# All head pairs turned on VectorE from long-run loads: a hashed attention followed by a channel mix on one core

## Chip, cores, metric

The kernel runs on one core of a Trainium2 chip. The metric is the device time of one execution in microseconds (us). A measurement is the median of several runs; profiles are of one execution.

## What is computed

Inputs q, k, v are 4 batches x 8 heads x 768 tokens x 64 values in float32. Each token of q and k gets a 6-bit bucket from the signs of six projections; attention runs only between tokens of one bucket. The result, with heads side by side (512 values per token), goes through a channel mix with a one-token shift.

```python
q_bits = (np.einsum('bhsd,dk->bhsk', q, proj) > 0)
mask = q_bucket[:, :, :, None] == k_bucket[:, :, None, :]
scores = np.where(mask, scale * (q @ k.T), -1e9)          # then softmax, then @ v
x = attn_out.transpose(0, 2, 1, 3).reshape(B, S, H * D)
x_prev = concatenate([zeros, x[:, :-1]], axis=1)
xk = mu_k * x + (1 - mu_k) * x_prev                        # xr alike, with mu_r
k = maximum(xk @ w_k, 0); v = k * k @ w_v                  # 512 -> 1024 -> 512
out = sigmoid(xr @ w_r) * v
```

## The kernel before

**Staging.** Two heads form a pair: 16 pairs, four per batch. A pair takes twelve slots, one for each head j and each block jc of 128 keys. The loop at L698 goes through all 192 slots; in each it records, for all engines, the score of that slot (`score`, L382: two matmuls and one exponential on ScalarE, L396), the product with v of the slot two earlier (`pv`, L404), some matmuls of the channel mix of the batch before (`ffn`, L580, from a list that is filled at slot 6 of the first pair of batches 1 to 3), and the steps that make later pairs ready. This text writes (n, s) for slot s of pair n. Every engine executes its own instructions in the order in which the loop recorded them, and so do the DMA queues of SP and ScalarE. After the loop come the rest of the list and the channel mix of the last batch, the tail.

**Masking by signs.** A score matmul contracts 64 values of a head and, in six further rows of the same operands (`augs`, called aq and ak in the profile), the signs of the projections as plus or minus a half. `bits` (L342) makes them: four matmuls of the turned pair with `projp`, one VectorE step to plus or minus a half into `sg`, and eight small SP DMAs (L360) that store six rows each into the operands.

**Turning.** q and k come in with tokens on partitions and must be turned to values on partitions (tile `t`). Pairs 0 to 3 (`NTE = 4`) are loaded naturally (`load_qk`, L235: 128 partitions of six tokens) and turned by TensorE transposes and bank copies (`turn_pe`, L305). Pairs 4 to 15 are loaded in blocks (`load_blocks`, L255) and turned by two VectorE transposes of 32 x 32 blocks (`turn_dve`, L326), with casts on GpSimd (L333). A block load puts, for one head and one half e of the 64 values, 32 rows of four runs of 352 values into 32 partitions; there are eight such DMAs a pair. `load_v` (L274) brings v of a pair in one DMA. Loads of pair n + 3 and of v of pair n + 2 stand at (n, 3).

**Output side.** `turn_out` (L437) turns a finished pair's result with TensorE into a PSUM bank, copies it to `xt`, and copies one column group for the shift. `mix` (L454) makes xk and xr of it in five VectorE steps. `rv_items` (L529) ends in `os` (L540) and one SP DMA of 128 rows x 2 KB. Squares (`norm`, L282) bound the scores; at the end a flag chooses a general path, which these inputs do not take.

**Weights** come through GpSimd's software queue (`load_w`, L591) at (0, 2), (0, 8), (1, 0), (1, 6), (1, 10) and (2, 10).

Of the kernel before, what the change touches and what calls it, by code (L numbers as in the profile page):

```python
# [9 lines left out]
FP32 = mybir.dt.float32  # L10
# [23 lines left out]
def kernel(  # L34
# [24 lines left out]
    NTE = 4  # L59
# [9 lines left out]
    projp = consts.tile([P, 32], FP32, name="projp")  # L69
# [99 lines left out]
    def fast():  # L169
        with ExitStack() as fx:  # L170
# [3 lines left out]
            nat = pool("nat", 3)  # L174
            blkp = pool("blk", 2)
            vfp = pool("vf", 3)
# [4 lines left out]
            ptp = pool("pt", 6)  # L181
# [9 lines left out]
            osp = pool("os", 4)  # L191
# [26 lines left out]
            nats, blks, vfs, pts, obs, xts, t32s, oos = ({} for _ in range(8))  # L218
# [16 lines left out]
            def load_qk(n):  # L235
                b, t = divmod(n, NPB)
                tl = nat.tile([P, 2, 2, HALF], FP32, name=f"qk{n}", tag="qk")
                nats[n] = tl
                if n == 0:
                    for j in range(2):  # L240
                        for i, eng in enumerate((nc.sync, nc.scalar)):
                            eng.dma_start(
                                out=tl[:, i, j, :],
                                in_=SRC[i][b, 2 * t + j].rearrange("(p c) d -> p (c d)", c=NC_),
                            )
                    return
                for i in range(2):
                    nc.sync.dma_start(
                        out=tl[:, i, :, :],
                        in_=SRC[i][b, 2 * t : 2 * t + 2].rearrange(  # L250
                            "j (p c) d -> p j (c d)", c=NC_
                        ),
                    )

            def load_blocks(n):  # L255

                b, t = divmod(n, NPB)
                tl = blkp.tile([P, 2, 4, HALF], FP32, name=f"bl{n}", tag="bl")
                blks[n] = tl
                w = HALF - D // 2  # L260
                for i in range(2):
                    for j in range(2):
                        src = SRC[i][b, 2 * t + j].rearrange("(f r c) d -> r f (c d)", f=4, c=NC_)
                        for e in range(2):
                            g = 2 * j + e
# [5 lines left out]
            def load_pair(n):  # L271
                (load_qk if n < NTE else load_blocks)(n)

            def load_v(n):  # L274
                b, t = divmod(n, NPB)
                vf = vfp.tile([P, 2, S // 2], FP32, name=f"vf{n}", tag="vf")
                nc.sync.dma_start(
                    out=vf, in_=v[b, 2 * t : 2 * t + 2].rearrange("j (p c) d -> p j (c d)", c=NC_)
                )
                vfs[n] = vf  # L280

            def norm(n, i, eng):  # L282

                if n < NTE:
                    src = nats[n][:, i].rearrange("p j f -> p (j f)")
                    shape = [P, S]
                else:
                    src = blks[n][:, i].rearrange("p f (c x) -> p (f c) x", x=D)[:, :, 0 : D // 2]
                    shape = [P, 4 * NC_, D // 2]
# [15 lines left out]
            def turn_pe(n, i, j, which):  # L305

                tp = bank(which, [P, HALF], FP32, f"tp{n}_{i}_{j}")
                for x in range(3):
                    cols = slice(x * P, (x + 1) * P)
                    nc.tensor.transpose(tp[:, cols], nats[n][:, i, j, cols], ident32)  # L310
                dst = t32(n)[:, i, j, :]
                if n == 0 and i == 1:
                    nc.scalar.copy(dst, tp)
                else:
                    nc.vector.tensor_copy(dst, tp)
                for e in range(2):
                    (nc.gpsimd, nc.vector)[e ^ j].tensor_scalar(
                        out=augs[n % NSET]["qk"[i], j][ROWS[j], e * HALF : (e + 1) * HALF],
                        in0=dst[ROWS[e], :],
                        scalar1=(1.0, ALPHA)[i],  # L320
                        scalar2=1.0,
                        op0=ALU.mult,
                        op1=ALU.mult,
                    )

            def turn_dve(n, i):  # L326
                src = blks[n][:, i].rearrange("p f (c x) -> p c f x", x=D)[:, :, :, 0 : D // 2]
                nc.vector.transpose(  # L328
                    t32(n)[:, i].rearrange("p h (c f x) -> p (h c) f x", c=3, f=4), src
                )  # L330

            def cast(n, i, j, eng):
                eng.tensor_scalar(  # L333
                    out=augs[n % NSET]["qk"[i], j][ROWS[j], :],
                    in0=t32(n)[ROWS[j], i].rearrange("p h y -> p (h y)"),
                    scalar1=(1.0, ALPHA)[i],
                    scalar2=1.0,
                    op0=ALU.mult,
                    op1=ALU.mult,
                )  # L340

            def bits(n, js, which, two_queues=False):  # L342


                bb = bank(which, [64 * len(js), HALF], FP32, f"bb{n}_{js[0]}")
                for g, (x, i) in enumerate((x, i) for x in js for i in range(2)):
                    nc.tensor.matmul(  # L347
                        bb[32 * g : 32 * g + 32, :], projp, t32(n)[:, i, x, :],
                        start=True, stop=True,
                    )  # L350
                sg = sgp.tile([64 * len(js), HALF], BF16, name=f"sg{n}_{js[0]}", tag="sg")
# [3 lines left out]
                for g, (x, i) in enumerate((x, i) for x in js for i in range(2)):  # L355
                    eng = nc.scalar if two_queues and i else nc.sync
                    for y in range(2):
                        j, e = (x, y) if n < NTE else (y, x)
                        r = 32 * g + NB * y
                        eng.dma_start(  # L360
# [3 lines left out]
                            in_=sg[r : r + NB, :],  # L364
                        )

            def values(n, j):
                vf = vfs[n][:, j, :]
                va, vs = vas[n % NSET][j], vss[n % NSET][j]
                if n < NTE:  # L370
                    to = va[:, :, 0:D].rearrange("p (e c) d -> p e c d", e=2)
                    of = vf.rearrange("p (c e d) -> p e c d", e=2, d=D)
                else:
                    to, of = va[:, :, 0:D], vf.rearrange("p (c d) -> p c d", d=D)
# [62 lines left out]
            def turn_out(n, which):  # L437
                b, t = divmod(n, NPB)
                xt = xtp.tile([P, P + S], BF16, name=f"xt{n}", tag=f"xt{t}")
                ot = bank(which, [P, S], BF16, f"ot{n}")  # L440

                for i in range(NC_):
                    c = 2 * (i % 3) + i // 3 if n < NTE else i
                    nc.tensor.transpose(ot[:, c * P : (c + 1) * P], obs[n][:, i, :], ident16)  # L444
                nc.vector.tensor_copy(xt[:, P : P + S], ot)  # L445
                xts[b, t] = xt

                nc.vector.memset(xt[:, 0:1], 0.0)
                nc.vector.tensor_copy(xt[:, 1:P], xt[:, S : S + P - 1])
# [4 lines left out]
            def mix(b, dc):  # L454

                xt = xts[b, dc]
                x, xp = xt[:, P : P + S], xt[:, 0:S]
                df = dfp.tile([P, S], BF16, name=f"df{b}_{dc}", tag="df")
                ops = [lambda: nc.vector.tensor_tensor(df, x, xp, op=ALU.subtract)]
                for i, nm in enumerate(("xk", "xr")):  # L460
# [3 lines left out]
                    ops += [  # L464
                        lambda m=m, mu=mu: nc.vector.tensor_scalar(
                            out=m, in0=df, scalar1=mu, scalar2=None, op0=ALU.mult
                        ),
                        lambda m=m: nc.vector.tensor_tensor(out=m, in0=m, in1=xp, op=ALU.add),  # L468
                    ]
# [59 lines left out]
            def rv_items(b, c):  # L529
# [8 lines left out]
                def v_done(vp):  # L538
                    os_ = osp.tile([P, DM], FP32, name=f"os{b}_{c}", tag="os")
                    nc.vector.scalar_tensor_tensor(  # L540
                        out=os_, in0=box["th"], scalar=1.0, in1=vp, op0=ALU.add, op1=ALU.mult
                    )
                    nc.sync.dma_start(
                        out=out[b].rearrange("(p c) m -> c p m", c=NC_)[c], in_=os_
                    )
# [55 lines left out]
            nc.sync.dma_start(out=projp[0:D, 0:NB], in_=proj)  # L601
            nc.scalar.dma_start(out=projp[D:P, NB : 2 * NB], in_=proj)
            load_qk(0)
# [3 lines left out]
            load_qk(1)  # L607
            load_v(0)
            idle = scp.tile([P, 2, 512], FP32, name="idle", tag="sc")
            for _ in range(8):  # L610
                nc.tensor.matmul(
                    idle[:, 0, 0:HALF],
                    epsm,
# [333 lines left out]
```

## Time and profile before

| | us |
|---|---|
| median of 3 runs (lowest, highest) | 275.41 (274.57, 276.19) |
| the profiled execution | 275.77 |
| its span in the profile | 274.0 |
| busy: PE / ScalarE / VectorE / GpSimd | 246.7 / 197.8 / 184.9 / 114.5 |
| exponentials, 192 of 812 ns | 150.7 |
| first exponential starts | 14.19 |
| first exponential of pair 4 starts | 61.45 |
| last exponential starts | 232.96 |
| last output step (L540) ends | 266.03 |

PE is TensorE's matmul row, PEld its weight loads, DVE is VectorE, ACT ScalarE, POOL GpSimd, SP the engine that issues most DMAs; "SPq" rows are DMA issues. In the page's second part each digit is a fortieth of the span in tenths of busy time. A DMA is cut into packets, one for each contiguous run, that sixteen DMA engines move; the DMA share is their mean busy time. In rows of groups and of the timeline, out<-in stands with partitions x elements.

### The profile page before, as it was taken

How to read it: one execution, taken by the hardware profiler on the slowest of the kernel's cores; microseconds unless marked ns; L12 is line 12 of the kernel's file. 1: busy time of each engine (PE TensorE's matmuls, PEld its weight loads, DVE VectorE, ACT ScalarE, POOL GpSimd, SP SyncE). 2: the span in 40 equal slices, each digit the busy share in tenths (PEclk: the TensorE clock that was granted, in tenths of full speed). 3: DMA queues.
4: the chain of work that ended last, by engine and by line, in shares of the span. 5: the costliest groups of instructions: out<-in, count | busy, mean ns of one | idle time of the engine just before them, and what ended most of it. 6: DMA issues, size and time to landing. Idle time of an engine off the chain costs nothing. (4 is left out here: it accounts for less than half of the span.)

```text
span 274.0 us, 6566 instructions
## 1 busy us (share of the span) xinstructions
PE 246.7 (90%) x2373; PEld 145.2 (53%) x2395; DVE 184.9 (67%) x412; ACT 197.8 (72%) x308; POOL 114.5 (42%) x210
## 2 busy tenths in 40 slices
PE   7888996777998999999989999999989999899970
PEld 3355763535564555556556556465655566454430
DVE  3566886698989683849798746568896535695220
ACT  3287985759787897878888888889788878267110
POOL 4489530977835726252546344454517000000000
PEclk9999999999999999999999999999999999999995
DMA  5379798799659286675957292928410112110321
GB/s 178 113 255 223 121 209 180 170 199 218 165 118 219 51 177 178 148 204 143 210 120 156 74 250 78 234 99 211 122 60 6 40 41 77 42 38 0 117 92 34
DMA packets 27736, 36.76 MB, mean 134 GB/s; under 512 B 3368, under 2 KB 24112, under 8 KB 27696
## 3 DMA queue, kind: packets, MB, share of 16 engines
q1 hardware_dynamic: 25136, 33.23, 47.3%
q0 software_dynamic: 2144, 2.62, 5.8%
q8 instruction: 21, 0.34, 0.5%
q10 hardware_dynamic: 416, 0.41, 0.5%
q14 instruction: 19, 0.16, 0.2%
HBM read 31.99 MB, written 6.29 MB: 140 GB/s over the span
## 5 line engine op out<-in xcount | busy, mean ns | idle before, releaser
L396 ACT ACTIVATE pt<-sc 128x768 bf16<-128x768 f32 x192 | 150.7, 812 | 40.9 <-PE sc L389 36.2
L389 PE MATMUL sc<-aq,ak 70*128 70x384 bf16 (+1 forms) x384 | 93.8, 325 | 3.9 <-ACT pt L396 2.7
L416 PEld LDWEIGHTS <-pt 128*128 128x128 bf16 x1152 | 60.6, 97 | 26.3 <-issue 1.1
L416 PE MATMUL oo<-va,pt 128*128 128x65 bf16 x1152 | 66.3, 193 | 0.0
L488 PE MATMUL kp<-xk,wk_sb 128*128 128x384 bf16 x256 | 53.1, 326 | 2.3 <-DVE xk L468 1.6
L488 PE MATMUL vp<-wv_sb,k 128*128 128x512 bf16 x176 | 50.5, 379 | 0.8 <-DVE os L540 0.2
L389 PEld LDWEIGHTS <-ak 70*128 70x128 bf16 (+1 forms) x384 | 34.3, 98 | 30.9 <-issue 9.3
L333 POOL TENSOR_SCALAR aq<-t 64x768 bf16<-64x768 f32 x24 | 19.9, 828 | 45.0 <-DVE t L328 44.0
L375 POOL CAST va<-vf 128x384 bf16<-128x384 f32 x32 | 16.5, 517 | 34.2 <-DMA vf<-in_v_dram 33.9
L540 DVE SCALAR_TENSOR_TENSOR os<-th,vp 128x512 f32<-128x512 bf16 x24 | 16.4, 685 | 20.2 <-PE vp L488 14.4
L488 PEld LDWEIGHTS <-wk_sb 128*128 128x128 bf16 x256 | 21.7, 97 | 14.9 <-issue 5.1
L524 DVE TENSOR_TENSOR k<-kr 128x384 bf16<-128x384 bf16 x64 | 27.5, 435 | 2.0 <-ACT kr L518 0.6
L488 PE MATMUL rp<-wr_sb,xr 128*128 128x512 bf16 x90 | 26.9, 379 | 0.3
L328 DVE STREAM_TRANSPOSE t<-bl 128x768 f32<-128x768 f32 x24 | 22.3, 957 | 2.2 <-DMA bl<-in_k_dram 2.2
L347 PE MATMUL bb<-t,projp 128*32 128x384 f32 x128 | 18.5, 509 | 4.9 <-DVE t L328 3.6
L535 ACT ACTIVATE th<-rp 128x512 bf16<-128x512 f32 x24 | 14.2, 594 | 11.9 <-PE rp L488 11.9
L488 PEld LDWEIGHTS <-k 128*128 128x128 bf16 x192 | 16.0, 97 | 11.3 <-issue 1.5
L445 DVE COPY xt<-ot 128x768 bf16<-128x768 bf16 x16 | 8.9, 557 | 18.9 <-PE ot L444 18.9
L333 POOL TENSOR_SCALAR ak<-t 64x768 bf16<-64x768 f32 x24 | 20.2, 843 | 2.4 <-DVE t L328 0.5
L377 POOL TENSOR_TENSOR s<-vf 128x192 f32<-128x192 f32 x32 | 21.1, 659 | 0.0
L520 DVE TENSOR_SCALAR kr<-kp 128x384 bf16<-128x384 f32 x32 | 17.6, 550 | 3.3 <-PE kp L488 3.1
L518 ACT ACTIVATE kr<-kp 128x384 bf16<-128x384 f32 x32 | 15.7, 492 | 5.7 <-PE kp L488 5.5
(62 smaller groups left out, 235.0 us busy)
## 6 DMA issues: line engine op xcount, KB each, us to landing
bl<-in_q_dram SPq DMA_DIRECT2D x48, 176.0 KB
bl<-in_k_dram SPq DMA_DIRECT2D x48, 176.0 KB
vf<-in_v_dram SPq DMA_DIRECT2D x16, 384.0 KB
out_dram<-os SPq DMA_DIRECT2D x24, 256.0 KB
qk<-in_q_dram SPq DMA_DIRECT2D x3, 384.0 KB
qk<-in_k_dram SPq DMA_DIRECT2D x3, 384.0 KB
aq<-sg SPq DMA_DIRECT2D x64, 4.5 KB
wk_sb<-in_moe_w_k_dram POOLq DMA_DIRECT2D x2, 512.0 KB, 6.0
```

Of the source, the lines that this page charges most:

```text
L328: nc.vector.transpose(t32(n)[:, i].rearrange("p h (c f x) -> p (h c) f x", c=3, f=4), src)
L333: eng.tensor_scalar(out=augs[n % NSET]["qk"[i], j][ROWS[j], :], in0=t32(n)[ROWS[j], i].rearrange("p h y -> p (h y)"), scalar1=(1.0, ALPHA)[i],
L347: nc.tensor.matmul(bb[32 * g : 32 * g + 32, :], projp, t32(n)[:, i, x, :], start=True, stop=True,)
L375: nc.gpsimd.tensor_copy(to, of)
L377: nc.gpsimd.tensor_add(s3, vf[:, 0 : 3 * D], vf[:, 3 * D : 6 * D])
L389: nc.tensor.matmul(sc[:, sp, 0:HALF], au["k", j][kr, jc * P : (jc + 1) * P], au["q", j][kr, sp * HALF : (sp + 1) * HALF], start=True, stop ...
L396: nc.scalar.activation(pt.rearrange("p (s q) -> p s q", s=2), sc[:, :, 0:HALF], AF.Exp, bias=EXP_BIAS, scale=SCALE,)
L416: nc.tensor.matmul(oo[:, ic, :], pts[n, j, jc][:, ic * P : (ic + 1) * P], vas[n % NSET][j][:, jc, :], start=False, stop=(jc == NC_ - 1 and ...
L488: nc.tensor.matmul(box["t"], lhs(), rhs(), start=(i == 0), stop=(i == len(mms) - 1))
L520: nc.vector.tensor_scalar(out=kr, in0=kp, scalar1=0.0, scalar2=None, op0=ALU.max)
L524: 1, lambda: nc.vector.tensor_tensor(out=k2, in0=kr, in1=kr, op=ALU.mult)
L540: nc.vector.scalar_tensor_tensor(out=os_, in0=box["th"], scalar=1.0, in1=vp, op0=ALU.add, op1=ALU.mult)
```

## The change

- All pairs are loaded in blocks and turned on VectorE. For one head, a block load is one DMA: two halves of the token's values, 32 rows, one run of 1,504 values (24 tokens less half a token) each, into 64 partitions; four DMAs a pair. Tokens are ordered r, f, c instead of f, r, c, so that a row's 24 tokens lie together in memory.
- v, one DMA a head, and the outputs follow that token order: the side in memory steps over f (4), then r (32).
- Pair 0 is loaded by head on two queues; the first head's signs are written by VectorE straight into the operands, the second head's by four DMAs.
- The mix takes its difference from PSUM and makes xk and xr in one fused step each; the shifted column group is two copies from PSUM.
- Loads move: pairs 1 and 2 ahead of the loop, 3 at (0, 4), 4 at (1, 2), 5 at (2, 2), then n + 3 at (n, 10); v at (n, 5). Weights move to (1, 8), (2, 8), (4, 2), (4, 8), (5, 2). Bits of pairs 2 to 5 stand at (n - 1, 1).
- Squares of pair n - 3 stand in (n, 5) and (n, 9) on ScalarE from pair 4 on, the last three pairs in the tail. Block buffers 2 to 6, v 3 to 2, exponentials 6 to 5, outputs 4 to 3. The very last output goes in two halves on two queues. The branch at the end names the other block as the one that follows.

```diff
-                            nc.sync.dma_start(
-                                out=tl[32 * g : 32 * g + 32, i, :, 0:w],
-                                in_=src[:, :, e * D // 2 : e * D // 2 + w],
-                            )      # src: "(f r c) d -> r f (c d)", 8 DMAs a pair
+            def rows(src, **kw):
+                return src.rearrange("(r f c) d -> f r (c d)", f=4, c=NC_)
+
+            def load_block(to, src, eng):
+
+                w = 4 * HALF - D // 2
+                eng.dma_start(
+                    out=to[:, 0:w],
+                    in_=bass.AP(
+                        tensor=src.tensor,
+                        offset=src.offset,
+                        ap=[[D // 2, 2], [4 * HALF, 32], [1, w]],
+                    ),
+                )
...
+            def load_first():
+
+                tl = blkp.tile([P, 2, 4 * HALF], FP32, name="bl0", tag="bl")
+                blks[0] = tl
+                for j in range(2):
+                    load_block(tl[0:D, j, :], SRC[0][0, j], nc.sync)
+                    load_block(tl[D:P, j, :], SRC[1][0, j], nc.scalar)
...
+                for i in range(2):
+                    for j in range(2):
+                        load_block(tl[D * j : D * j + D, i, :], SRC[i][b, 2 * t + j], nc.sync)
...
-                nc.sync.dma_start(
-                    out=vf, in_=v[b, 2 * t : 2 * t + 2].rearrange("j (p c) d -> p j (c d)", c=NC_)
-                )
+                for j in range(2):
+                    nc.sync.dma_start(out=vf[:, j, :], in_=rows(v[b, 2 * t + j]))
...
-                ops = [lambda: nc.vector.tensor_tensor(df, x, xp, op=ALU.subtract)]
+                ops = [lambda: nc.vector.tensor_tensor(df, ot, xp, op=ALU.subtract)]
...
+                    ops.append(
+                        lambda m=m, mu=mu: nc.vector.scalar_tensor_tensor(
+                            out=m, in0=df, scalar=mu, in1=xp, op0=ALU.mult, op1=ALU.add
+                        )
+                    )
...
-                    nc.sync.dma_start(
-                        out=out[b].rearrange("(p c) m -> c p m", c=NC_)[c], in_=os_
-                    )
+                    parts = 2 if b == B - 1 and c == NC_ - 1 else 1
...
+                        (nc.scalar if x < parts - 1 else nc.sync).dma_start(
+                            out=out[b].rearrange("(r f c) m -> c f r m", f=4, c=NC_)[c][:, :, y],
+                            in_=os_[:, y],
+                        )
...
+            keep_warm(12)
+            turn_dve(0, 0)
+            cast_first(0, 0, nc.gpsimd)
+            cast_first(1, 0, nc.scalar)
+            b0 = bits_first(0, "A")
+            keep_warm(6)
+            turn_dve(0, 1)
...
+            signs_first(b0, 0, 0)
+            signs_first(b0, 1, 0)
+            signs_first(b0, 0, 1)
...
+            LOADS = {(0, 4): (3,), (1, 2): (4,), (2, 2): (5,)}
```

More of the change, by code (lines that the diff above doesn't have):

```diff
@@ new lines, in load_block @@
+            def load_block(to, src, eng):
[14 more added lines that the diff above has]
+                    load_block(tl[D:P, j, :], SRC[1][0, j], nc.scalar)
+                    if j == 0:
+                        nc.sync.dma_start(out=projp[0:D, 0:NB], in_=proj)
+                        nc.scalar.dma_start(out=projp[D:P, NB : 2 * NB], in_=proj)
@@ L303, in t32, with cast_first, bits_first, signs_first @@
                 return t32s[n]
[L305 to L323, printed above, removed]
-                    )
+            def cast_first(i, j, eng):
+                cast_op(augs[0]["qk"[i], j][ROWS[j], :], t32(0)[ROWS[i], j], i, eng)
+            def bits_first(j, which):
+                bb = bank(which, [P, HALF], FP32, f"bb0_{j}")
+                for g, (e, i) in enumerate(STRIPS):
+                    nc.tensor.matmul(
+                        bb[32 * g : 32 * g + 32, :],
+                        projp[ROWS[i], NB * i : NB * i + 32],
+                        t32(0)[ROWS[i], j, e, :],
+                        start=True, stop=True,
+                    )
+                return bb
+            def signs_first(bb, e, i):
+                g = 2 * e + i
+                signs(
+                    augs[0]["qk"[i], 0][SROWS[0], e * HALF : (e + 1) * HALF],
+                    bb[32 * g : 32 * g + NB, :],
+                )
             def turn_dve(n, i):
-                src = blks[n][:, i].rearrange("p f (c x) -> p c f x", x=D)[:, :, :, 0 : D // 2]
+                src = blks[n][:, i].rearrange("p (f c x) -> p c f x", f=4, x=D)[:, :, :, 0 : D // 2]
                 nc.vector.transpose(
@@ L330, in turn_dve, with cast_op, signs @@
                 )
-            def cast(n, i, j, eng):
[L333 to L351, printed above, removed]
+            def cast_op(to, t, i, eng):
+                of = t.rearrange("p h y -> p (h y)")
+                if eng is nc.scalar:
+                    eng.activation(to, of, AF.Copy, scale=(1.0, ALPHA)[i])
+                    return
+                eng.tensor_scalar(
+                    out=to, in0=of, scalar1=(1.0, ALPHA)[i], scalar2=1.0,
+                    op0=ALU.mult, op1=ALU.mult,
+                )
+            def cast(n, i, j, eng):
+                cast_op(augs[n % NSET]["qk"[i], j][ROWS[j], :], t32(n)[ROWS[j], i], i, eng)
+            def signs(sg, bb):
                 nc.vector.tensor_scalar(
@@ L354, in bits, with store_signs @@
                 )
[L355 to L360, printed above, removed]
+            STRIPS = [(e, i) for e in range(2) for i in range(2)]
+            def bits(n, which):
+                bb = bank(which, [P, HALF], FP32, f"bb{n}")
+                for g, (e, i) in enumerate(STRIPS):
+                    nc.tensor.matmul(
+                        bb[32 * g : 32 * g + 32, :], projp[:, 0:32], t32(n)[:, i, e, :],
+                        start=True, stop=True,
+                    )
+                store_signs(n, bb, ((0, 0), (1, NB)))
+            def store_signs(n, bb, heads):
+                sg = sgp.tile([P, HALF], BF16, name=f"sg{n}", tag="sg")
+                signs(sg, bb)
+                for g, (e, i) in enumerate(STRIPS):
+                    for j, at in heads:
+                        nc.sync.dma_start(
                             out=augs[n % NSET]["qk"[i], j][
@@ L598, in load_w @@
                 )
-            nc.sync.dma_start(out=projp[0:D, 0:NB], in_=proj)
-            nc.scalar.dma_start(out=projp[D:P, NB : 2 * NB], in_=proj)
-            load_qk(0)
+            load_first()
             warm = rcp.tile([P, 1], FP32, name="warm", tag="warm")
@@ new lines, in fast, with keep_warm @@
+            for x, src in enumerate((moe_mu_k, moe_mu_r)):
+                nc.scalar.dma_start(
+                    out=mu_rows[x * NDC : (x + 1) * NDC, :],
+                    in_=src.rearrange("(c p) -> c p", p=P),
+                )
+            idle = scp.tile([P, 2, 512], FP32, name="idle", tag="sc")
+            def keep_warm(count):
+                for _ in range(count):
+                    nc.tensor.matmul(
+                        idle[:, 0, 0:HALF],
+                        epsm,
+                        epsm[:, None, :].to_broadcast([P, 3, P]),
+                        start=True,
+                        stop=True,
+                    )
@@ L687, in squares @@
             def squares(n, s):
[L688 to L695 removed]
+                if n >= NPB and s in (5, 9):
+                    norm(n - 3, s // 9, nc.scalar)
             pieces = []
@@ L702, in fast @@
                 run_due()
-                if live and s == 3:
-                    if n + 3 < NPAIRS:
-                        load_pair(n + 3)
-                    if n + 2 < NPAIRS:
+                if live:
+                    for m in LOADS.get((n, s), (n + 3,) if n >= 3 and s == 10 else ()):
+                        if m < NPAIRS:
+                            load_blocks(m)
+                    if s == 5 and n + 2 < NPAIRS:
                         load_v(n + 2)
@@ L770, in check_bound @@
                 )
-            for n in range(1, NTE):
+            for n in range(NPAIRS - 3, NPAIRS):
                 for i in range(2):
-                    later(3 + 4 * n + 2 * i, lambda n=n, i=i: norm(n, i, nc.scalar))
+                    later(6 + 4 * (n - NPAIRS + 3) + 2 * i, lambda n=n, i=i: norm(n, i, nc.scalar))
             later(22, check_bound)
```

178 lines of the change are left out of this document (58 added, 120 removed).

## The prediction

> **What bounds the kernel now.** I read the page first, then the busy table cut at the points where the work changes kind, then ScalarE's timeline, then the DMA tables.
>
> ```profile
> span 274.0 us, 6566 instructions
> ...
> PE 246.7 (90%) x2373; PEld 145.2 (53%) x2395; DVE 184.9 (67%) x412; ACT 197.8 (72%) x308; POOL 114.5 (42%) x210
> ...
> DMA  5379798799659286675957292928410112110321
> ```
>
> By the averages TensorE is the bound and the sixteen DMA engines have air. The table by stage (columns: stretch, its length, busy time of PE, PEld, DVE, ACT, POOL, granted clock, DMA share, GB/s) says when each holds:
>
> ```profile
> 0.00:14.19 14.19, 11.08 (x41) 5.08 (x42) 6.29 (x29) 4.12 (x9) 7.08 (x21) 1.00 0.44 140
> 14.19:61.45 47.26, 39.71 (x471) 25.50 (x471) 35.94 (x75) 36.01 (x49) 29.76 (x56) 1.00 0.87 196
> 61.45:201.48 140.03, 133.76 (x1380) 80.48 (x1391) 104.87 (x224) 118.12 (x187) 70.96 (x124) 1.00 0.66 158
> 201.48:274.00 72.52, 62.19 (x487) 34.17 (x493) 37.81 (x88) 39.51 (x65) 6.76 (x12) 0.96 0.13 46
> ```
>
> 14.19 is the first exponential, 61.45 the first one of pair 4, 201.48 that of pair 13's slot 8. Batch 0 (row two) is the only stretch where no engine is full and the DMA engines nearly are; from pair 4 on PE is at 96%. ScalarE's timeline shows batch 0's stalls, in brackets at the first exponentials of pairs 3 and 4:
>
> ```profile
> 48.40 2.25 ACT L396 ACTIVATE pt<-sc 128x768 bf16<-128x768 f32 x3 [3.35 <-PE sc L389]
> ...
> 61.45 0.81 ACT L396 ACTIVATE pt<-sc 128x768 bf16<-128x768 f32 x1 [3.18 <-PE sc L389]
> ```
>
> So there are about 14 us of lead-in and 6.5 us of stalls that loads can win or lose. Now the DMA view:
>
> ```profile
> DMA packets 27736, 36.76 MB, mean 134 GB/s; under 512 B 3368, under 2 KB 24112, under 8 KB 27696
> ## 3 DMA queue, kind: packets, MB, share of 16 engines
> q1 hardware_dynamic: 25136, 33.23, 47.3%
> ...
> q10 hardware_dynamic: 416, 0.41, 0.5%
> ...
> bl<-in_q_dram SPq DMA_DIRECT2D x48, 176.0 KB
> ...
> aq<-sg SPq DMA_DIRECT2D x64, 4.5 KB
> ```
>
> **How a DMA is dealt over the engines.** Queue q1 is SP's. Its DMAs carry, one packet per contiguous run: 96 block loads of 32 x 4 runs = 12,288; 16 v loads of 128 x 2 = 4,096; six natural q/k loads of 256 and two of 128 = 1,792; 24 outputs of 128 = 3,072; 124 sign stores of 6 = 744; proj 64; the two mu rows 4 each = 8. That is 22,064 of 25,136, so 3,072 packets are no data. They fit one finishing packet per engine that took part: 16 for each of 145 DMAs with 32, 64 or 128 outer rows (2,320), 6 for each sign store of six rows (744), 4 for each mu load (8); the sum is 3,072 exactly. ScalarE's queue q10 gives 344 data packets and 72 = 3 x 16 + 4 x 6. So in this profile a DMA is shared out by whole steps of its outermost dimension: 6 rows go to 6 engines, 4 rows to 4.
>
> Every DMA here has the same outermost count on both sides. The change breaks that. A block load now reads 2 x 32 runs of 1,504 values (the outer 2 is the half of a token) into 64 partitions; a v load reads 4 x 32 rows into 128; an output writes 4 x 32 rows from 128. A share of whole outer steps on both sides leaves 2 engines for a block load and 4 for v and the outputs. No run here shows such an unlike pair; that is the weak point, and the first rival takes the other side of it.
>
> The Trainium skill has this as a rule (DMA: Bandwidth & Descriptors, section "Why a DMA increments its semaphore by 16 and not by 1"): the engine count is the largest number up to 16 that divides the slowest dimension above one of both access patterns. The 6 and the 4 above agree; by the rule the counts would be 2 and 4, and the sum would be the one below.
>
> **What one engine moves.** The block loads now run slowly though all engines are busy, other transfers faster:
>
> ```profile
> 17.00:22.00 5.00, 4.91 (x61) 3.16 (x54) 3.28 (x8) 4.18 (x6) 4.62 (x10) 1.00 1.04 372
> ...
> 38.00:41.00 3.00, 2.81 (x40) 2.04 (x39) 2.24 (x7) 2.99 (x5) 0.00 (x0) 1.00 1.09 220
> ...
> 262.00:263.00 1.00, 1.00 (x7) 0.47 (x5) 0.25 (x1) 0.00 (x0) 0.00 (x0) 1.00 0.40 152
> ```
>
> Rate over share over 16: 22.4 GB/s per engine for 1,536-byte packets (natural loads), 23.8 for 2,048-byte ones (an output), 12.6 for block loads, where sixteen engines write into one stripe of 32 partitions. From the first two a packet takes 68.6 and 86.1 ns, so about 16 ns plus 0.034 ns a byte; a 6,016-byte packet would take 222 ns, 27.1 GB/s. Two engines do not crowd a stripe, so I take 25, between 23.8 and 27.1; the ends 22.4 and 27.1 are kept.
>
> **The sum on the first two engines**, which serve every block load, v load and output, through pair 15's load:
> - block loads: 16 pairs x 4 DMAs x 32 packets x 6,016 B at 25 GB/s (241 ns) = 493 us (455 at 27.1, 550 at 22.4). One pair takes 31 us; before, eight DMAs of 176 KB at 220 GB/s took 6.6.
> - v of pairs 0 to 14 goes ahead of it: 15 x 64 packets x 68.6 ns = 66.
> - twelve outputs of batches 0 and 1: 12 x 32 x 86 ns = 33.
> - weights on the software queue, whose share of 5.8% of 274 us is 16 on each engine; signs and finishing packets about 8.
> - first packet about 2 us after the start.
>
> That is 618 us. I looked for holes in this queue. In the built program's SP order each block load stands behind at most an output whose VectorE step precedes the turn of the pair still loading, or waits only for that pair's first half; so the next load is always queued. A turn takes 1.9 us (two at 957 ns), far less than a load.
>
> Pair 15 is turned at slot 8 of pair 13. From there the work is that of before: 72.5 us (last row of the stage table). The tail's outputs, each 32 x 86 ns = 2.75 us on four engines, just exceed the 2.6 us between their VectorE steps, and the last one, halved on two queues but on the same engines, ends about 2 us later than now: +2.5. The profiled execution took 275.77 for a span of 274.0, so 1.8 more, and the median of 275.41 lies 0.4 lower. 618 + 72.5 + 2.5 + 1.4 = 694 us.
>
> **The other parts.** Under such loads they are covered: PE, DVE and ACT need 12 to 15 us per pair (140 us for nine pairs and more) of the 36 that the loads take. Their size without that cover matters for the first rival:
> - Turning pairs 0 to 3 on VectorE drops 48 PE transposes (8.9 us) and 14 bank copies (7.7), adds 8 turns (7.7); PE and DVE are not full in batch 0.
> - First head's signs written in place: three 0.55 us VectorE steps in place of a 2 us store; head 1's store now queues behind pair 1's load.
> - Mixes: 2.77 us now (694 + 484 + 596 + 434 + 564 ns). After: a subtraction that reads PSUM (557 to 932, by the copy of that shape and by the one-pass square of L295) and two fused steps near L295's 932: 2.4 to 2.8. Nothing.
> - The shifted column by two copies in place of one of 302 ns: 0 to +0.3 each on DVE.
> - Weights later, squares later, fewer output buffers: hidden; the end branch may move the last 6 us by 1 or 2 either way.
> - The wait that the change adds: VectorE now waits for loads at each turn, with the evictions and FFN steps of the same slots behind it, and PE behind those. That is how the load time reaches the end.
>
> **Rivals.**
> 1. All sixteen engines serve a load, dealt by the 64 partitions of its target: faster. First head: 770 KB at 320 GB/s (the rate from 3 to 9 us) land at 5.4, the second at 7.8, a turn, three sign steps, a score: first exponential near 11 in place of 14.2. Batch 0's 6.5 us of stalls shrink, less about 2 because pair 1's bits wait for a load twice as large: 270 us. It decides if the target's rows alone set the deal. For it: 32-, 64- and 128-row DMAs all show 16. Against: both sides must be cut alike, and 2 outer steps cannot be cut in 16.
> 2. Sixteen engines, but block loads keep the 220 GB/s of today, and batch 0 now carries six of them, 9.2 MB, in place of four natural and fewer block pairs: about 56 us with v and weights before pair 4 can go, against 47: 280 us.
> 3. Two engines, each at the 12.6 GB/s of today's block loads because the reading, not the stripe, is slow: 493 becomes 978, total near 1,180.
>
> **How the numbers follow.** Two engines at 22 to 27 GB/s 0.85, rival 1 0.09, rival 2 0.03, rival 3 0.03. The likeliest alone gives 655 to 751; if v and outputs sit on other engines than the block loads, up to 90 less; if a load has to wait for its predecessor's turn some ten times, at 3 us, 30 more. So 600 to 785 us holds a little over 8 in 10. About 0.5% (1.4 us) is what a measurement of this kernel can tell from no change. Faster 0.09, same 0.01, slower 0.90.
>
> **What would show it.** Right: far fewer finishing packets (2 per block load, 4 per v load and output), a DMA share near 2/16 at about 50 GB/s for most of the span, block loads landing some 31 us per pair, DVE's longest wait the turn for the load of bl, PE busy under half, first exponential of the kernel after 35 us. Wrong: a DMA share over 0.5 in batch 0, or pair 4 before 70 us; then rival 1 or 2 holds.

## The result, and the profile after

The changed kernel takes 735.8 us (median of four runs, 735.57 to 738.41) beside 275.8 us (274.57 to 276.26) for the kernel before on the same chip: a ratio of 2.672, 95% interval 2.661 to 2.683. Ratios here and below leave out executions that lie more than 1.5% above the fastest of the same kernel. The profiled execution took 735.57 us, its span is 733.7.

The page of the changed kernel, lines that answer to those of before. The clock digits are tenths of full speed, one for each fortieth of the span:

```profile
span 733.7 us, 6452 instructions
...
PE 293.0 (40%) x2343; PEld 153.7 (21%) x2365; DVE 173.8 (24%) x370; ACT 201.3 (27%) x315; POOL 116.1 (16%) x208
...
PEclk7555657575757659576575857759585856858997
DMA  1111111121212313111111211111111211111212
...
DMA packets 15578, 40.90 MB, mean 56 GB/s; under 512 B 1348, under 2 KB 7988, under 8 KB 15540
...
q1 hardware_dynamic: 13052, 36.90, 14.0%
```

Every engine is idle for more than half of the span, and the DMA engines together are busy one to three tenths of any slice (0.17 in most stages), though 40.90 MB are moved and not 36.76. By stage (columns as in the stage table of before; 39.60 is the first exponential, 227.50 that of pair 4, 659.50 the second turn of pair 15):

```profile
0.00:39.60 39.60, 9.62 (x37) 3.21 (x38) 5.73 (x24) 4.20 (x7) 4.97 (x17) 0.65 0.14 50
39.60:227.50 187.90, 46.37 (x437) 26.41 (x436) 27.07 (x51) 36.42 (x49) 31.33 (x56) 0.60 0.17 56
227.50:659.50 432.00, 176.60 (x1432) 91.72 (x1443) 105.86 (x217) 123.40 (x195) 74.69 (x127) 0.68 0.17 57
659.50:733.70 74.20, 60.38 (x442) 32.32 (x450) 35.12 (x80) 37.32 (x65) 5.08 (x10) 0.91 0.17 50
```

Until the last pair is turned the DMA share stays at 0.14 to 0.17, near 2/16, at 50 to 57 GB/s; the stage after it is as long as it was (74.2 us for 72.5). The waits (engine, line waited for: us in total, times, longest) show how the load time reaches the engines: VectorE's turn (L319 now) waits for a block load, ScalarE for the scores behind it.

```profile
ACT pt L390 <- PE sc L383: 381.0, 83, 30.8
...
DVE t L319 <- DMA bl<-in_k_dram: 201.9, 15, 15.0
DVE t L319 <- DMA bl<-in_q_dram: 179.5, 13, 19.4
```

How the DMAs are dealt follows from q1's row as it did before. Its data packets are 62 block loads of 64, 32 v loads of 128, 23 outputs of 128 and half an output of 128, 124 sign stores of 6, and 64 of projp: 3,968 + 4,096 + 2,944 + 128 + 744 + 64 = 11,944. The row has 13,052, so 1,108 packets are no data: 62 x 2 + 32 x 4 + 24 x 4 + 124 x 6 + 16. So a block load finishes on two engines, v and an output on four.

### The profile page after: what moved, and what is told of

It is laid out like the page before. It is cut to its first block, busy times and chain, and to the rows that moved or that the text cites. A ratio compares the mean times of both kernels' runs of the same rounds, so it can differ in the third digit from the quotient of the medians.

```text
span 733.7 us, 6452 instructions
## 1 busy us (share of the span) xinstructions
PE 293.0 (40%) x2343; PEld 153.7 (21%) x2365; DVE 173.8 (24%) x370; ACT 201.3 (27%) x315; POOL 116.1 (16%) x208
## 2 busy tenths in 40 slices
DMA packets 15578, 40.90 MB, mean 56 GB/s; under 512 B 1348, under 2 KB 7988, under 8 KB 15540
## 3 DMA queue, kind: packets, MB, share of 16 engines
q1 hardware_dynamic: 13052, 36.90, 14.0%
## 4 chain that ended last, share of the span: by engine, by line
## 5 line engine op out<-in xcount | busy, mean ns | idle before, releaser
L383 PE MATMUL sc<-aq,ak 70*128 70x384 bf16 (+1 forms) x384 | 106.3, 362 | 117.9 <-DMA ak<-sg 114.6
L347 PE MATMUL bb<-t,projp 128*32 128x384 f32 x120 | 38.9, 848 | 253.9 <-DVE t L319 253.9
L319 DVE STREAM_TRANSPOSE t<-bl 128x768 f32<-128x768 f32 x32 | 31.3, 978 | 441.6 <-DMA bl<-in_k_dram 201.9
L410 PEld LDWEIGHTS <-pt 128*128 128x128 bf16 x1152 | 67.1, 104 | 33.3 <-issue 11.5
L410 PE MATMUL oo<-va,pt 128*128 128x65 bf16 x1152 | 72.6, 203 | 0.1
L347 PEld LDWEIGHTS bb<-t,projp 128*32 128x32 f32 x120 | 4.9, 140 | 272.6 <-DVE t L319 271.3
L328 POOL TENSOR_SCALAR aq<-t 64x768 bf16<-64x768 f32 x32 | 26.5, 827 | 220.5 <-DVE t L319 219.1
L328 POOL TENSOR_SCALAR ak<-t 64x768 bf16<-64x768 f32 x31 | 25.8, 831 | 152.6 <-DVE t L319 138.4
L283 ACT ACTIVATE sq<-bl 128x768 bf16<-128x768 f32 x32 | 26.9, 840 | 11.7 <-DMA bl<-in_q_dram 11.7
L538 DVE SCALAR_TENSOR_TENSOR os<-th,vp 128x512 f32<-128x512 bf16 (+1 forms) x25 | 16.4, 658 | 16.4 <-PE vp L483 9.8
```

The costliest lines, as they stand in the source:

```text
L283: nc.scalar.activation(junk, src, AF.Square, accum_out=acc)
L319: nc.vector.transpose(t32(n)[:, i].rearrange("p h (c f x) -> p (h c) f x", c=3, f=4), src)
L328: eng.tensor_scalar(out=to, in0=of, scalar1=(1.0, ALPHA)[i], scalar2=1.0, op0=ALU.mult, op1=ALU.mult,)
L347: nc.tensor.matmul(bb[32 * g : 32 * g + 32, :], projp[:, 0:32], t32(n)[:, i, e, :], start=True, stop=True,)
L383: nc.tensor.matmul(sc[:, sp, 0:HALF], au["k", j][kr, jc * P : (jc + 1) * P], au["q", j][kr, sp * HALF : (sp + 1) * HALF], start=True, stop ...
L410: nc.tensor.matmul(oo[:, ic, :], pts[n, j, jc][:, ic * P : (ic + 1) * P], vas[n % NSET][j][:, jc, :], start=False, stop=(jc == NC_ - 1 and ...
```

## The experiments

Theory A is that of the prediction: a DMA is shared out by whole steps that both sides have, two for a block load. Its rivals had all sixteen engines serve a load (270 us, or 280 with slow block loads), or two slow ones (1,180 us). The expectations add theory B, that the long runs or their overlapping reads are slow in themselves, and theory C, that SP is held back by few DMAs in flight. Ratios are to the kernel before, run beside each kernel (medians of 276.3 to 276.8 us). A kernel with one run has no interval. Line numbers differ by a few from kernel to kernel.

### The deal alone, in the kernel before

Block loads of the kernel before, recut: runs stay at 1,408 bytes, eight DMAs a tensor and pair, but each reads 2 x 32 runs into 64 partitions in place of 32 x 4 into 32.

```diff
...      # src is no longer rearranged
-                        for e in range(2):
-                            g = 2 * j + e
+                        for f in range(4):
                             nc.sync.dma_start(
-                                out=tl[32 * g : 32 * g + 32, i, :, 0:w],
-                                in_=src[:, :, e * D // 2 : e * D // 2 + w],
+                                out=tl[D * j : D * j + D, i, f, 0:w],
+                                in_=bass.AP(... ap=[[D // 2, 2], [HALF, 32], [1, w]]),
```

> The kernel before, with one thing changed: each of its block loads takes both halves of one run group, 2 x 32 runs into 64 partitions, instead of one half of four groups, 32 x 4 runs into 32; the same 1,408-byte runs, 16 DMAs a pair instead of 8. Theory A: the loads of pairs 4 to 15 go to two engines, 512 packets of about 62 ns each per pair, 32 us, 35 with holes: 12 x 35 from about 36 us on, and 72 after it: 500 to 560 us. Theory B: the runs are as before, so within 5 us of before plus up to 10 for SP's issues.

Measured: 538.97 us, one run. Nothing of the rest of the change is in it. The page, and the first of its waits:

```profile
DMA  4881212211212112112131121121311311311112
...
POOL va L378 <- DMA vf<-in_v_dram: 346.5, 12, 34.2
```

The share falls from eight tenths to one to three where the block loads begin, at about 40 us. Its 12,288 block packets take 64 ns each in the mean (100 ns in the kernel before): 12,288 x 64 / 2 = 393 us on each of two engines, against 428 us from the first of them (37.6) to the last (465.2). So the outermost 2 by itself nearly doubles the time, and the long runs have no part in it. Each of the two engines moves a packet faster than each of the sixteen did (64 ns for 100), as the prediction took it, but two of them are not sixteen.

### The deal undone, step by step, in the changed kernel

First only q's block loads in two DMAs of 32 rows each, k's as they are:

```diff
+                if src.tensor is q.tensor:
+                    for e in range(2):
+                        eng.dma_start(out=to[32 * e : 32 * e + 32, 0:w], in_=... ap=[[4 * HALF, 32], [1, w]])
+                    return
```

> The changed kernel with only q's block loads dealt by 32 rows; k's stay at 2 x 32. Theory A: engines 0 and 1 keep k (14.8 us a pair), v (4.2) and a sixteenth of q, 21 to 25 us a pair with holes, so 450 to 510 us. Theory B or C: above 650.

Measured: 544.86 us, one run. It lies between, as theory A has it, but above its figure; the last block load lands at 467 us. Then both tensors so (this kernel is e1 in the next expectations):

```diff
-                eng.dma_start(out=to[:, 0:w], in_=... ap=[[D // 2, 2], [4 * HALF, 32], [1, w]])
+                for e in range(2):
+                    eng.dma_start(out=to[32 * e : 32 * e + 32, 0:w], in_=... ap=[[4 * HALF, 32], [1, w]])
```

> The changed kernel, but each block load is two DMAs, one for each half of the token's values, whose outermost count is 32 on both sides; runs of 1,504 values, order, schedule and everything else stay, v and outputs still step over 4 first. Theory A (a DMA is dealt over engines by the outermost counts, 2 before, 32 now): the 29.6 us of block loads per pair fall to about 7 and the kernel to 265 to 290 us, with first exponential near 11 us instead of 39.6. Theory B (the long runs of 6 KB, or their overlapping reads, are slow in themselves): still above 650 us. Theory C (SP is held back by few DMAs in flight, whatever they are): eight DMAs a pair instead of four, no faster than 735.

Measured: 366.13 us (365.0 to 368.44), ratio 1.324 [1.320, 1.328]. Half the time is gone with this edit alone, first exponential at 12.7 us in place of 39.6. The figure was missed by 76 us and more. The waits, first of all engines and then of SP's queue, say where:

```profile
POOL va L370 <- DMA vf<-in_v_dram: 123.4, 28, 13.2
```

```profile
SPq L241 <- DMA vf<-in_v_dram: 70.2, 24, 4.5
```

SP's issue of a block load (L241) is held 24 times, 70.2 us in all, until v's transfer, still on four engines, has ended (why it waits for v is told further down). So v and outputs go by 32 rows as well:

```diff
-                for j in range(2):
-                    nc.sync.dma_start(out=vf[:, j, :], in_=rows(v[b, 2 * t + j]))
+                for f in range(4):
+                    nc.sync.dma_start(out=vf[32 * f : 32 * f + 32, :, :], in_=src[f])
...      # src: "j (r f c) d -> f r j (c d)"
+                        for f in range(4):     # and an output alike
```

> As e1, and v (four DMAs a pair of 32 partitions, both heads) and outputs (four DMAs of 32 rows) are dealt by 32 too. Theory A: v and outputs on four engines cost 4.2 and 2.7 us of those engines per pair and per output, mostly hidden behind PE once block loads are quick; 2 to 8 us less than e1, most of it in batch 0 and at the last output (about 2). If four engines were no limit: within 1 us of e1, or slower by the extra issues on SP (0.4 us each).

Measured: 296.72 us (293.54 to 297.15), ratio 1.075 [1.072, 1.077]. The edit that was to bring 2 to 8 us brings 69, and SP's wait for v falls from 70.2 us to 1.1. With block loads, v and outputs all on sixteen engines the changed kernel is still 20 us behind. Two of ScalarE's idle times (in brackets, with what ended them), before pairs 3 and 4:

```profile
55.89 0.81 ACT L394 ACTIVATE pt<-sc 128x768 bf16<-128x768 f32 x1 [5.76 <-PE sc L387]
...
70.85 1.51 ACT L394 ACTIVATE pt<-sc 128x768 bf16<-128x768 f32 x2 [3.23 <-PE sc L387]
```

From the first exponential (13.0) to that of pair 4 are 57.8 us, 47.3 in the kernel before. That is the second rival's 56 us, and its slow block loads are there: a block packet takes 411 ns (median) here and 229 ns when two engines serve it, 14.6 and 26.3 GB/s for each engine. Whether its cause holds too is not shown: the DMA share in these 57.8 us is 0.73, less than the 0.87 of the kernel before, and SP is busy issuing for 45 of them. By the start of pair 15 (235.8 for 220.6) the lag is 15 us.

### Where the sum of the prediction failed

In the changed kernel pair 15's load landed at 659 us, forecast 618. Block packets have a size of their own (6,016 bytes), so the packets' starts and durations in the traces split the time into stretches from the first to the last block packet of a pair ("in loads") and those between pairs:

| kernel | in loads | between | of it without a v or output packet | last one lands |
|---|---|---|---|---|
| changed | 520.1 | 136.7 | 33.6 | 659.0 |
| changed, v and outputs on sixteen | 542.5 | 92.0 | 47.0 | 636.7 |
| changed, signs by GpSimd | 520.9 | 61.3 | 0.0 | 584.4 |
| v and outputs on sixteen, signs by GpSimd | 538.8 | 28.8 | 5.4 | 569.7 |

The first of these rows shows stretches without any load, which the prediction had excluded. SP's timeline in the changed kernel (start, length of the issues in us) shows what stands there:

```profile
379.79 8.48 SPq L358 DMA_DIRECT2D aq<-sg  x2
388.32 1.36 SPq L358 DMA_DIRECT2D ak<-sg  x2
389.73 1.96 SPq L358 DMA_DIRECT2D aq<-sg  x2
398.19 3.12 SPq L358 DMA_DIRECT2D ak<-sg  x2
401.41 0.62 SPq L542 DMA_DIRECT2D out_dram<-os  x1
402.13 1.57 SPq L273 DMA_DIRECT2D vf<-in_v_dram  x2
403.80 1.10 SPq L542 DMA_DIRECT2D out_dram<-os  x1
405.00 4.60 SPq L240 DMA_DIRECT2D bl<-in_q_dram  x2
```

The loads of a pair end at 397.7. Only then do the last sign stores (L358) of the pair before go out, and v, the outputs and the next load stand behind them; that load's first packet moves at 413.7. The trace's semaphores say why. The DMAs of SP and ScalarE take eight completion semaphores in turn, and 238 of SP's 243 wait, before they are issued, until their own is free, that is, until the DMA that used it last, nearly always the eighth before, has landed. The eight sign stores of a pair follow the four block loads and an output, so the sixth and seventh store wait for k's two loads: those land at 390.96 and 398.17, the stores go at 391.02 and 398.19. This is a wait that the program states, and it is the one that held e1's block loads of k behind v.

Second row: v and outputs by 32 rows with the edit shown above, block loads left on two engines.

> The changed kernel with its block loads as they are (two engines each), but v by four DMAs of 32 rows a pair and each output by four DMAs of 32 rows, so that these are dealt over all sixteen engines. If the terms of the sum add on the first two engines (the theory of the prediction, with the sizes now measured): v of 15 pairs falls from 70 us to a quarter, the twelve outputs from 43 us to a quarter, so some 85 us less than 736: 640 to 665 us. If the block loads alone set the time and the holes come from SP's queue whatever v does: over 700. If v's price on four engines is one of waiting in SP's queue, as it seemed to be when the block loads had sixteen engines (70 us there): 650 to 680, hard to tell from the first.

Measured: 711.79 us, one run. 24 us less, not 85: the terms do not add, as the second case of the expectation had it. Third row: only the queue of the sign stores is changed.

```diff
                     for j, at in heads:
-                        nc.sync.dma_start(
+                        nc.gpsimd.dma_start(
```

> The changed kernel with one edit: the sign stores are issued by GpSimd on its software queue and not by SP. In the trace of the changed kernel SP is held at the issue of a pair's last sign stores until the next pair's loads have drained (issues of 6 to 16 us), so that the load after that starts 3 us or more after the last one ended. If these holes, some 20 us until pair 15's load, are what the sum missed beside the sizes of its terms: 710 to 722 us, pair 15's load landed near 640 (669 by my forecast's arithmetic plus sizes is the upper end of it). If the holes are only where other terms would lie (the first engines are the bound all the same): 730 to 742.

Measured: 661.95 us, one run; 74 us less, far beyond either figure. The edit also gives the stores eight semaphores of GpSimd's own, so that SP's eight now span a pair's loads, v and outputs alone; more semaphores for SP were not tried. SP's waits, first of the changed kernel and then of this one:

```profile
SPq L358 <- DMA bl<-in_k_dram: 134.5, 25, 8.1
```

```profile
SPq L542 <- DVE os L538: 31.6, 9, 5.5
SPq L273 <- POOL vs L373: 26.5, 4, 10.9
SPq L542 <- DVE rc L421: 24.5, 1, 24.5
SPq L240 <- DMA bl<-in_k_dram: 19.0, 2, 17.0
```

The row of 134.5 us is gone. In the table the time in loads is the same to 0.8 us; all of the gain lies between the pairs, 75.4 us: 33.6 were empty, and the other 42 are v and outputs, which now overlap with block packets. Fourth row, both edits:

> The same edit on the kernel with v and outputs dealt over sixteen engines (712 us). There the busy time of the first two engines up to pair 15's load adds up to some 587 us (block packets 527, v 22, outputs 12, weights 16, signs and the start 10) and the load landed at 637, so 50 us are holes. If SP's held issue makes them: 655 to 675, and the sum without holes is right again. If not: 700 to 715.

Measured: 646.34 us, one run: 65 us less than with SP's stores. The direction is confirmed twice; the size was too small, by 48 us and more in the first and by 9 to 29 in the second, since I had counted as holes only time in which no block packet and none of v or the outputs moved.

### The other parts of the change, each in the kernel before

Each of these moves the time by about 1% or less.

Weights later:

```diff
-                0: {2: ("k", 0, 2), 8: ("k", 2, 2)},
-                1: {0: ("v", 0, 4), 6: ("v", 4, 4), 10: ("r", 0, 2)},
-                2: {10: ("r", 2, 2)},
+                1: {8: ("k", 0, 2)}, 2: {8: ("k", 2, 2)},
+                4: {2: ("r", 0, 4), 8: ("v", 0, 4)},
+                5: {2: ("v", 4, 4)},
```

> The kernel before with the weights' loads moved to (1, 8), (2, 8), (4, 2), (4, 8) and (5, 2), as in the change, and nothing else. The prediction called this hidden under slow loads; in the kernel before, where the DMA engines are 87% busy in batch 0 and 6.5 us of stalls there wait for loads, the bytes taken out of batch 0 (about 2.6 MB of 9.3) should shorten the stalls: 1 to 5 us faster, 270.5 to 274.5. If the stalls of batch 0 come from the order in SP's queue and not from bytes: 275 to 276.

Measured: 273.47 us beside 276.34, ratio 0.991 [0.987, 0.995]. Its stages, cut at the same events as those of before:

```profile
0.00:13.33 13.33, 9.67 (x41) 4.19 (x42) 6.20 (x29) 4.13 (x9) 7.10 (x21) 1.00 0.45 150
13.33:58.46 45.13, 39.59 (x471) 25.57 (x471) 35.88 (x75) 35.85 (x48) 27.66 (x51) 1.00 0.68 168
```

Batch 0 is 2.1 us shorter and its DMA share falls from 0.87 to 0.68; the lead-in is 0.9 shorter. The time falls within the first case, but the two stalls that it names shrink by only 0.7 us, from 6.53 to 5.86 (2.35 ahead of pair 3, 3.51 ahead of pair 4); the rest of the 2.1 lies before them. This version has the lowest median of all here.

The mix in three operations:

```diff
-                ops = [lambda: nc.vector.tensor_tensor(df, x, xp, op=ALU.subtract)]
+                ops = [lambda: nc.vector.tensor_tensor(df, ot, xp, op=ALU.subtract)]
...      # tensor_scalar and tensor_tensor become one scalar_tensor_tensor
```

> The kernel before with the mix in three operations, the difference read from PSUM, as in the change. The prediction's price is 2.4 to 2.8 us in place of 2.77 for each of 16 mixes, so nothing: 274.5 to 276.5. Rival: VectorE is not full (67%), but the PSUM bank is held longer, until the difference is taken, and PE at 96% from pair 4 on waits for the bank: 1 to 3 us slower.

Measured: 274.74 us, ratio 0.994 [0.990, 0.998], 0.6% faster. The groups (busy us, mean ns of one):

```profile
L465 DVE SCALAR_TENSOR_TENSOR xk<-df,mu_sb,xt 128x768 bf16<-128x768 bf16 x16 | 16.8, 1053 | 0.6
L465 DVE SCALAR_TENSOR_TENSOR xr<-df,mu_sb,xt 128x768 bf16<-128x768 bf16 x16 | 16.3, 1018 | 0.0
L459 DVE TENSOR_TENSOR df<-ot,xt 128x768 bf16<-128x768 bf16 x16 | 8.9, 554 | 0.3
```

554 + 1,053 + 1,018 ns = 2.63 us for one mix, within the 2.4 to 2.8 of the prediction; no wait for the bank stands among PE's waits.

The first head's signs written in place, the second head's stores all on SP:

```diff
-                bits(0, (j,), "AC"[j], two_queues=True)
+                if j == 0:
+                    bits_direct("A")      # four VectorE steps into augs[0]
+                else:
+                    bits(0, (j,), "AC"[j])
```

> The kernel before with one part of the change: the signs of the first head of pair 0 are written by VectorE straight into the operands (four steps, three columns of strips), no store, and the second head's stores go by SP alone. The prediction put the store at about 2 us of the lead-in of 14.19 us and let PE-bound pairs from pair 4 on carry the rest: if the path to the first exponential runs through the stores, it starts at 11 to 12 us and the time falls by 2 to 3 us, to 272.5 to 273.5. If batch 0 is bound by loads, pair 1 waits for its own signs all the same and the time stays at 275 to 276 though the first exponential is earlier.

Measured: 277.3 us, ratio 1.006 [1.002, 1.009]: 0.6% slower, which neither case had. The first exponential starts at 13.36 us, earlier than 14.19, but not than the 13.33 of the kernel with only its weights moved. v and the loads of pair 2 now stand on SP behind four stores of the second head and not two (issued from 14.9 us on), and pair 3 starts at 51.0 us (48.4 before). That the stores cause this was not tried alone.

Weights later and the mix together, and the bits of pairs 4 and 5 at (n - 1, 1) as in the change:

```diff
-                if n and s == 1 and n + 1 < NTE:
+                if n and s == 1 and n + 1 < NPB + 2:
...
-                    if s == 11:
+                    if s == 11 and m >= NPB + 2:
```

> The kernel before with three parts of the change together: weights later, the mix in three operations, and the bits of pairs 4 and 5 at (n - 1, 1), so that TensorE is not held at the end of pairs 2 and 3 by bits that wait for a turn that waits for a load. Alone the first two measured 0.991 and 0.994. If the stalls ahead of pairs 3 and 4 (2.4 and 3.5 us with weights later) come from that order on TensorE: 4 to 8 us faster than before, 267 to 271. If the loads themselves are late (the turn at pair 4's start waits all the same): 271 to 273.

Measured: 274.96 us beside 276.75, ratio 0.996 [0.993, 1.000]. Both figures were missed, and the gains of the parts do not add. ScalarE still waits ahead of pairs 3 and 4, and again after pair 3's second score:

```profile
46.95 0.81 ACT L396 ACTIVATE pt<-sc 128x768 bf16<-128x768 f32 x1 [2.56 <-PE sc L389]
...
50.09 7.37 ACT L396 ACTIVATE pt<-sc 128x768 bf16<-128x768 f32 x10 [1.36 <-PE sc L389]
59.25 1.51 ACT L396 ACTIVATE pt<-sc 128x768 bf16<-128x768 f32 x2 [1.78 <-PE sc L389]
```

Moving the bits on TensorE has not removed them. With the loads of pairs 4 and 5 put ahead of the signs of pairs 2 and 3 as well:

```diff
+                if live and s == (0 if n in (1, 2) else 3) and n + 3 < NPAIRS:
+                    load_pair(n + 3)
                 if live and s == 3:
-                    if n + 3 < NPAIRS:
-                        load_pair(n + 3)
```

> The kernel of the run before this one with the block loads of pairs 4 and 5 issued at (1, 0) and (2, 0), ahead of the signs of pairs 2 and 3 in SP's order, and not behind them at (1, 3) and (2, 3). With weights later the DMA share in pair 1 is 0.12, so there is room. If late loads are the rest of batch 0's stalls: 1 to 4 us less than the run before this one. Rival: the signs of pairs 2 and 3 now queue behind 1.4 MB of loads, some 6.6 us, and pairs 2 and 3 start later: 1 to 4 us more.

Measured: 278.55 us as the median of ten runs that spread from 273.43 to 282.31, ratio 0.994 [0.990, 0.999]. With such a spread, whether this helps is not settled.

## Why the prediction was right, and where its sum was not

- **Deal.** Right. 1,108 finishing packets where 3,072 were, 2 for a block load and 4 for v and outputs; the recut loads nearly doubled the time of the kernel before, and dealing block loads, v and outputs by 32 rows took 735.8 to 296.7. By the Trainium skill's rule (DMA: Bandwidth & Descriptors, section "Why a DMA increments its semaphore by 16 and not by 1") the counts are 2 and 4, and the trace agrees with these 1,108 packets.
- **Block loads, 493 us.** Measured 520 in loads, 5% more: the packet's median is 229 ns (241 forecast), but some packets take longer, and the mean is 244. That one engine moves 6 KB packets at 25 GB/s, far from the 12.6 of sixteen, was right, and the third rival with it wrong.
- **v, outputs, weights, signs, 123 us on the first engines.** Too large: with the sign stores off SP, all that lies between the loads of the pairs is 61 us. So these transfers lie beside the block loads more than a plain sum on the first two engines has them.
- **"The next load is always queued".** This is the step that failed. I followed the order of the loads in SP's program and asked what each must wait for, but passed over the sign stores among them and the eight semaphores that all these DMAs share: the stores wait for the loads ahead to land, and every later load waits behind the stores. It costs 75 us. Without it the load would land at 584, below the 618 of the forecast; with it, at 659. Two errors of opposite sign, 62 too much and 75 too little, and 27 in loads, leave the 41 us by which the landing was late; that the total came within 6% is in part luck. The 30 us that the forecast kept aside for loads that wait for a turn were for another cause.
- **After the last load.** 72.5 + 2.5 forecast, 74.7 from the landing to the end of the span.
- **What hides the other parts.** PE is busy 40% of the span, the first exponential starts at 39.6 us, VectorE's longest wait is the turn: as listed. Taken alone they are worth -2.9 us (weights), -1.6 (mix) and +1.0 (signs) by the medians, 1% at the most.
- **The rivals at sixteen engines.** No run dealt a load into 64 partitions over sixteen engines, which is what these two describe; the nearest one, with 32 partitions a load, takes 296.7, well above the first one's 270. The second one's batch 0 of 56 us is close to what that kernel shows (57.8), its 280 us is short by 17: pair 15 starts 15 us late, and the end of the span is 18 us late. Where the part after batch 0 is lost was not followed further. One candidate is SP itself, which issues 409 DMAs there for 271 before, and is busy issuing for 113 of the 130 us from 70.85 to 201 (98.6 of 140 us in the same stage before).

## What to carry to other kernels

Before a DMA is reshaped for longer runs, compare the outermost counts of its two sides, and count the packets without data in the profile to see how many engines serve it: here fewer, longer runs at twice the rate of one engine lost to two engines in place of sixteen. Look then at every small DMA between two large ones in the same queue: one that must wait there, here for the completion semaphore of the DMA eight before it, holds up all that stands behind it. Where a sum over a queue is made, test its "no holes" with the stretches between the transfers before trusting its total.

## What was not expected of the hardware

- Beside the program's own wait for a semaphore (134.5 us at sign stores in the changed kernel, 25 times, 8.1 us the longest), SP can be long in the issue itself: 56 of its 243 DMA issues take over 1.5 us, 361 us in all, where the kernel before has three of 271, 5 us in all. The issue of k's second load at 364.05, for one, takes 8.44 us though its semaphore came free at 357.5. How much may be open before that begins was not measured.
- Four engines for v and outputs cost 24 us (735.8 to 711.8) beside block loads on two, and 69 us (366.1 to 296.7) beside block loads on sixteen, where SP was held for 70.2 us behind v.
- In the changed kernel the granted clock falls to 0.60 in batch 0 and 0.68 after it, against 1.00 in the same stages before, while PE is idle for more than half of the time; the matmuls of the bits take 848 ns each, 509 before. What this costs was not measured apart: the loads set the time of those stages, and the stage after the last load, where the clock is 0.91 for 0.96, is within 2 us of its length before.
